# Sigmoid attention with mixture of depths on one core: rankings, choosing, turns, stores and weight loads given other places in a hand-written order

## The chip, the core and the metric

The kernel runs on one core of a Trainium2 chip. The core has a matrix engine (PE, with its weight loads shown apart as PEld), a vector engine (DVE), a scalar engine (ACT), a general engine (POOL), a queue engine for transfers (SP), and 16 DMA engines between on-chip memory and HBM. Each engine works through its own list of instructions strictly in the order written, and waits where an instruction needs what another engine or a transfer has not yet delivered. The metric is the device time in microseconds (us).

## What is computed

Inputs are q, k and v of shape (8, 12, 448, 64), a gate vector of 768 and two weights, 768 x 1024 and 1024 x 768. All is float32.

```python
scores = scale * np.matmul(q, k.transpose(0, 1, 3, 2)) - np.log(S)
attn = 1.0 / (1.0 + np.exp(-scores))
x = np.matmul(attn, v)             # then (B, H, S, D) -> (B, S, H*D)
scores = np.einsum('bsd,d->bs', x, w_gate)
out = x.copy()
for b in range(B):
    top_idx = np.argpartition(-scores[b], capacity)[:capacity]   # 128 of 448
    xe = x[b, top_idx]
    ye = np.maximum(xe @ w1, 0.0) @ w2
    g = 1.0 / (1.0 + np.exp(-scores[b, top_idx]))
    out[b, top_idx] = x[b, top_idx] + g[:, None] * ye
```

So each batch first needs its attention, then a score for each token, then the rank of each token, and only for the 128 best tokens the two layers.

## The kernel before

**Attention.** The 96 heads are worked in 12 units s = 0 to 11 of two groups of four heads. Three groups make a batch, so batch b is complete after unit (3b+2)//2, and `FULL[b]` names the unit after that one: 2, 3, 5, 6, 8, 9, 11, 12. Each unit has 7 slots n = 0 to 6. A slot (`slot`, L322, L351) scores two row blocks of its own unit into the banks PA (`a0`, `a1`), lets ACT squash them (`squash`, L336) into attn tiles, and beside this accumulates values (`value`) of slots 0 to 3 for the unit before it and of slots 4 to 6 for its own unit, into the banks PO (`o0`, `o1`). The last values of a unit fall in slot 3 of the next, and there DVE takes the result out of PO in four transposes (`takes`, L372). One round of values in a unit is odd: it holds two half rounds that write the same banks from different rows of the array, so that ACT puts a `join` (L359) between them. This is slot (s,3) from s = 4 on, and (s,2) for s = 1 to 3.

**Per batch.** After the takes, DVE multiplies and sums with the gate vector (`gate_part`, L380 and L383, for each group), `gate` (L398 to L413) makes the scores, and POOL sends them to HBM (L408). `spread` (L420, on POOL) brings them back as `rep`, the same row in all 128 partitions. `ranking` compares them (`rank`, L428 and L431, four blocks of tokens) and `place` (L441 to L456) builds a one-hot matrix, for batches 2 to 5 also sums of it. `choose` (L465, L469) multiplies that on PE, `fetch` (L476, L479) turns the answer into row numbers on DVE and starts the gather of 128 rows from `out` on POOL (L489). These rows must have been stored before: `store` (L389) writes x in four pieces of rows. `scatter` (L630) writes the finished rows back.

**The two layers.** They run for pairs of batches p. `turn_rows` (item `("t", b)`, L507 to L529) transposes the gathered rows. Each layer is done with 7 products instead of 8, on quarters of the weights and on sums of quarters: items `(1, p, key)` (`first`, L546, with sums on DVE or ACT at L559 to L565) and `(2, p, key)` (`second`, L610, with sums into the rows at L621); `("c", b)` is choose and fetch. Three quarters of each weight are held, the fourth and the four sums are made once (`make_sum`, L200), kept in HBM (L202) and lent again to a spare buffer when needed (`lend`, L225). The lists in `BLOCKS` say which items come after slot (s,3) of which unit; `block` hands each item a pair of banks or one half of a pair, two items in turn to each pair.

**Order.** The order is written out by hand: `after(s, n)` says what follows each slot, and every instruction is put on its engine's queue in that order. Buffers make the queues wait for each other. `raw_k` has one buffer, so the load of k 2s+4 waits until `turn` (L304) has turned k 2s+3. qT and kT have four buffers, so new ones wait until PE has finished an older unit. `rep` has one buffer, xe three. Loads (L101, L150, L177), lends, sums to HBM and stores all go through SP's one queue. After the last slot, `rest` does the remaining values, the last two batches and the last pair.

Of the kernel before, what the change touches and what calls it, by code (L numbers as in the profile page):

```python
# [17 lines left out]
def kernel(  # L18
# [161 lines left out]
    def load_held(m):  # L180
        for x, at in enumerate((HELD1, HELD2)[m - 1]):
            load_quarter(m, (w1_sb, w2_sb)[m - 1][:, x], at)
# [3 lines left out]
    def load_left(m):  # L186

        for n, x in ((1, "a"), (2, "b")):
            room[x] = spare(n)[:, :QW]
        load_quarter(m, room["a"], (1, 0) if m == 1 else (0, 1))  # L190

    def make_sum(m, key):
        a, b = room["a"], room["b"]
        w00, wx, w11 = [(w1_sb, w2_sb)[m - 1][:, x] for x in range(3)]
        dst, x, y, op = {
            (1, 5): (b, a, w11, ALU.add), (1, 7): (a, w00, a, ALU.subtract),
            (1, 6): (b, w11, a, ALU.subtract), (1, 3): (a, wx, b, ALU.subtract),
            (2, 5): (b, a, w00, ALU.subtract), (2, 7): (a, a, w11, ALU.subtract),
            (2, 6): (b, w00, a, ALU.subtract), (2, 4): (a, wx, b, ALU.subtract)}[m, key]
        nc.vector.tensor_tensor(out=dst, in0=x, in1=y, op=op)  # L200
        t = sums[m, key] = dram.tile([P, QW], F32, name=f"sum{m}{key}", bufs=1)
        nc.sync.dma_start(out=t, in_=dst)  # L202


    SUMS = {(1, 4): [(1, 5)], (1, 6): [(1, 7)], (2, 1): [(1, 6)], (2, 4): [(1, 3)],
            (4, 4): [(2, 5)], (4, 6): [(2, 7)], (5, 1): [(2, 6)], (5, 2): [(2, 4)]}
# [421 lines left out]
    def scatter(b):  # L628
# [8 lines left out]
        4: [("t", 0), (1, 0, 1), ("c", 1)],  # L637
        5: [("t", 1), (1, 0, 2), (1, 0, 6)],
        6: [(1, 0, 7), (1, 0, 4), (1, 0, 5), ("c", 2), (1, 0, 3), (2, 0, 1)],
        7: [(2, 0, 2), (2, 0, 4), (2, 0, 3), (2, 0, 5), (2, 0, 6), ("c", 3), ("t", 2)],  # L640
        8: [(2, 0, 7), ("t", 3), (1, 1, 1), (1, 1, 2), (1, 1, 6), (1, 1, 7), (1, 1, 4)],
        9: [(1, 1, 5), (1, 1, 3), (2, 1, 1), ("c", 4), (2, 1, 2), (2, 1, 4)],
        10: [(2, 1, 3), (2, 1, 5), (2, 1, 6), ("c", 5), (2, 1, 7), ("t", 4)],
        11: [(1, 2, 1), ("t", 5), (1, 2, 2)],
# [21 lines left out]
    def block(s):  # L666

        places = [("o0", 0), ("o0", 1), ("a1", 0), ("a1", 1), ("a0", 0), ("a0", 1),
                  ("o1", 0), ("o1", 1)]
        at = 0  # L670
        for i, item in enumerate(BLOCKS[s]):
            if item[0] == "t":
                at += at % 2
                turn_rows(item[1], banks(places[at % 8][0]))
                at += 2
            else:
                name, n = places[at % 8]
                ps = banks(name)[:, n]
                if item[0] == "c":
                    fetch(*choose(item[1], ps))  # L680
                else:
                    finish(item, begin(item, ps))
                at += 1
            if i == 1:
                turn("q", 2 * s + 2)
                turn("k", 2 * s + 3)
                load("k", 2 * s + 4)
            if i == 2:
                turn("q", 2 * s + 3)
# [36 lines left out]
    def slot(s, n):  # L726
# [11 lines left out]
        if split(vs, i):  # L738
            one, two, u = rounds(vs)[i]
            for e, p in ((0, one), (1, two)):  # L740
                for half in range(2):
                    if e == 0:
                        score(s, n, e, 1 - half, PA[1 - half])
                        value(vs, half, p, u)
                        join(half)
                    else:
                        value(vs, half, p, u)
                        score(s, n, e, 1 - half, PA[1 - half])
                        squash(s, n, 1 - half, PA[1 - half])
                        if i == 6:  # L750
                            takes(vs, half)
            return
        for half in range(2):
# [16 lines left out]
            if (s, n, half) == (FIRST - 1, NF + 1, 0):  # L770
                fetch(*choose(0, PO[1][:, 1]))

    FIRST = NG // 2 + 3

    def rest():
# [3 lines left out]
        ranking(B - 2)  # L779
# [56 lines left out]
    def after(s, n):  # L836

        if n == NF and s:
            if 4 < s:
                load_v(s)  # L840
            if s in BLOCKS:
                block(s)
            else:
                turn("q", 2 * s + 2)
                turn("k", 2 * s + 3)
                load("k", 2 * s + 4)
                turn("q", 2 * s + 3)
            gates(2 * s - 2)
            gates(2 * s - 1)
# [3 lines left out]
        if s == 0:  # L853
# [5 lines left out]
            if n == 3:  # L859
                load_held(1)  # L860
                load_left(1)
# [6 lines left out]
        if (s, n) in ((1, 4), (2, 6), (3, 4)):  # L868
            load_v({1: 2, 2: 3, 3: 4}[s])
        for key in SUMS.get((s, n), ()):  # L870
            make_sum(*key)
        if (s, n) == (4, 0):
            load_held(2)
            load_left(2)
        for b in range(B - 1):
            full = FULL[b]
            if (s, n) == (full, 5 + b % 2):
                spread(b)
            if (s, n) == (full, 6):
                store(b)  # L880
            if (s, n) == (full + 1, 1):
                ranking(b)
        if s == NS - 1:
# [3 lines left out]
            if n == 6:  # L887
                lend(2, 5, "heads")
                lend(2, 6, "heads")
                lend(2, 7, "attn")  # L890

# [55 lines left out]
```

## Time and profile before

The three runs took 543.79, 545.67 and 547.75 us, so the median is 545.67. The profiled execution took 542.69 us, of which its span on the core is 540.9.

| | busy us of 540.9 | share |
|---|---|---|
| PE | 456.9 | 84% |
| PE weight load | 258.6 | 48% |
| DVE | 305.3 | 56% |
| ACT | 188.4 | 35% |
| POOL | 33.2 | 6% |
| mean DMA, 84.67 MB | 157 GB/s | |
| granted PE clock, mean | 0.934 | |

The page gives busy shares; they are averages over stages with different limits. Where PE stands still is read from the list of waits and from the timelines: a line there has start and length in us, the engine, the line of the kernel, the operation with what it writes and reads, the number of instructions merged, and in brackets how long the engine was idle before and what ended that. The granted clock of PE is given for each stretch of time; 1.00 is full speed. Half speed makes a 2.7 us item of the first layer take 5.4.

### The profile page before, as it was taken

Reading aid. Unit: us, or ns where it says so; the run is one execution under the profiler, and the core shown is the slowest. Engines: PE = TensorE matmul, PEld = TensorE weight load, DVE = VectorE, ACT = ScalarE, POOL = GpSimd, SP = SyncE. Lnnn points to the kernel's source line nnn. Section 1 sums busy time; section 2 is a strip of 40 time slices with the busy share of each in tenths; the row PEclk is TensorE's granted clock in tenths of the full one; section 3 lists DMA queues with packets and bytes.
Section 4 is the critical chain, followed back from the end, with each engine's and each line's share of the span. In section 5 each row is a group of like instructions: output and inputs, shape, how many; then the busy total and the mean of one; then the engine's idle time right before and its main releaser. Section 6 shows DMA issues by size and latency. Waiting matters only on the chain.

```text
span 540.9 us, 14311 instructions
## 1 busy us (share of the span) xinstructions
PE 456.9 (84%) x6374; PEld 258.6 (48%) x6374; DVE 305.3 (56%) x643; ACT 188.4 (35%) x225; POOL 33.2 (6%) x55
## 2 busy tenths in 40 slices
PE   8999997089897967895899897769578999899995
PEld 3535332034546537332444842634134365877962
DVE  3329575626747584945542567446646065986462
ACT  4666663036362630351065055005402642000100
POOL 5000010010000000000000000000002000001001
PEclk9999998579899989997999999879978999799998
DMA  8986639799385892953643694158716378351001
GB/s 212 335 222 192 214 109 163 205 159 331 127 320 134 234 209 85 240 150 68 196 150 94 193 161 147 33 179 151 199 52 212 120 128 227 62 98 59 30 1 58
DMA packets 115726, 84.67 MB, mean 157 GB/s; under 512 B 90624, under 2 KB 99456, under 8 KB 115664
## 3 DMA queue, kind: packets, MB, share of 16 engines
q1 hardware_dynamic: 113680, 75.84, 53.3%
q0 software_dynamic: 1984, 7.91, 4.7%
q8 instruction: 50, 0.82, 0.6%
q14 instruction: 12, 0.10, 0.1%
HBM read 63.28 MB, written 20.46 MB: 155 GB/s over the span
## 4 chain that ended last, share of the span: by engine, by line
PE 56%; DVE 19%; DMA 10%; issue 7%; SPq 4%; ACT 2%; POOL 0%; POOLq 0%; DVEq 0%; ACTq 0%
PE a L322 14%; PE o L351 13%; PE o L546 8%; PE o L610 6%; PE a L546 6%; PE a L610 6%; DMA rep<-scores 4%; SPq L389 2%; DMA scores<-total 2%; DVE scr L431 2%; DVE scr L428 2%; ACT attn L336 2%; DVE hidden L559 2%; DVE x_b L372 2%; DVE xe L621 2%
## 5 line engine op out<-in xcount | busy, mean ns | idle before, releaser
L322 PE MATMUL a<-qT,kT 32*64 32x448 f32 x2624 | 256.5, 544 | 7.7 <-ACT attn L336 5.9
L336 ACT ACTIVATE attn<-a,bias_s 128x896 f32<-128x896 f32 x162 | 162.0, 1007 | 146.0 <-PE a L322 93.1
L351 PE MATMUL o<-attn,raw_v 32*64 32x448 f32 x2176 | 206.3, 541 | 0.2 <-issue 0.2
L322 PEld LDWEIGHTS a<-qT,kT 32*64 32x64 f32 x2624 | 92.1, 132 | 105.3 <-ACT attn L336 71.1
L351 PEld LDWEIGHTS o<-attn,raw_v 32*64 32x64 f32 x2176 | 73.6, 132 | 36.8 <-issue 30.2
L351 PE MATMUL o<-attn,rows_t 32*64 32x448 f32 x448 | 45.6, 565 | 19.8 <-DVE got L479 17.5
L372 DVE STREAM_TRANSPOSE x_b<-o 128x448 f32<-128x448 f32 x48 | 26.9, 616 | 43.2 <-PE a L322 33.1
L304 DVE STREAM_TRANSPOSE kT<-raw_k 128x448 f32<-128x448 f32 x42 | 24.2, 616 | 36.6 <-PE a L322 19.5
L428 DVE TENSOR_SCALAR_CACHE_REDUCE scr<-rep,who 128x448 f32<-128x448 f32 (+1 forms) x32 | 21.6, 676 | 33.4 <-DMA rep<-scores 32.5
L546 PE MATMUL o<-rows_t,spare 128*128 128x128 f32 x192 | 29.4, 323 | 10.3 <-DVE x_b L372 8.1
L562 ACT ACTIVATE hidden<-hidden 128x512 f32<-128x512 f32 x12 | 7.5, 630 | 80.1 <-DVE hidden L559 80.1
L546 PEld LDWEIGHTS o<-rows_t,spare 128*128 128x128 f32 x192 | 28.2, 236 | 12.2 <-DVE x_b L372 9.7
L351 PEld LDWEIGHTS o<-attn,rows_t 32*64 32x64 f32 x448 | 16.1, 136 | 31.3 <-DVE got L479 19.0
L296 DVE STREAM_TRANSPOSE qT<-qT 128x896 f32<-128x896 f32 x23 | 25.2, 1094 | 10.4 <-DMA qT<-in_q_dram 10.4
L383 DVE TENSOR_REDUCE gate_p<-scr 128x14 f32<-128x448 f32 x48 | 29.8, 621 | 1.7
L380 DVE TENSOR_TENSOR scr<-x_b,wg_b 128x448 f32<-128x448 f32 x48 | 29.7, 619 | 1.1
L610 PE MATMUL o<-w_sb,hidden 128*128 128x384 f32 x40 | 18.6, 621 | 12.7 <-DVE x_b L372 12.7
L621 DVE SCALAR_TENSOR_TENSOR xe<-a,gate,xe 128x384 f32<-128x384 f32 x32 | 18.1, 609 | 16.0 <-PE a L610 11.9
L510 ACT ACTIVATE rows_t<-o 128x768 f32<-128x768 f32 x4 | 3.2, 811 | 68.3 <-PE o L507 42.9
L559 DVE TENSOR_TENSOR hidden<-o,hidden 128x512 f32<-128x512 f32 x17 | 11.3, 687 | 24.6 <-PE o L546 24.5
L431 DVE SCALAR_TENSOR_TENSOR scr<-rep,who,earlier 128x448 f32<-128x448 f32 (+1 forms) x32 | 21.8, 683 | 1.4
L610 PE MATMUL a<-w_sb,hidden 128*128 128x384 f32 x56 | 21.3, 527 | 0.8 <-DVE hidden L559 0.8
(112 smaller groups left out, 417.2 us busy)
## 6 DMA issues: line engine op xcount, KB each, us to landing
spare<-sum SPq DMA_DIRECT2D x38, 384.0 KB, 4.4
qT<-in_q_dram SPq DMA_DIRECT2D x24, 448.0 KB, 6.2
out_dram<-x_b SPq DMA_DIRECT2D x32, 336.0 KB, 7.7
raw_k<-in_k_dram SPq DMA_DIRECT2D x22, 448.0 KB, 4.6
raw_v<-in_v_dram SPq DMA_DIRECT2D x36, 224.0 KB, 4.7
sum<-spare SPq DMA_DIRECT2D x8, 768.0 KB, 5.5
w_sb<-in_moe_w_dram SPq DMA_DIRECT2D x6, 768.0 KB, 10.3
rows_t<-in_v_dram SPq DMA_DIRECT2D x8, 224.0 KB, 10.6
```

Of the source, the lines that this page charges most:

```text
L296: nc.vector.transpose(heads["q", i], heads["q", i])
L322: nc.tensor.matmul(out[y * Dh:(y + 1) * Dh, h % 2, :S], kt[d, e, r:r + 2].rearrange("d r t -> d (r t)"), qt[d, e], start=(e == 0), stop=(e ...
L336: nc.scalar.activation(a, psc[:, :, :S], AF.Sigmoid, bias=bias_s, scale=QK_SCALE)
L351: nc.tensor.matmul(PO[x][j * Dh:(j + 1) * Dh, pr, :S], raw_v[s][rows, 2 * pr + j, at:at + Dh], attn[s, pr, n][rows, j, :], start=((s, x, p ...
L372: nc.vector.transpose(x_tiles[b][:, :, 2 * g + pr, :], PO[x][:, pr, :S].rearrange("p (r t) -> p r t", t=TT))
L380: nc.vector.tensor_tensor(out=tmp, in0=x_tiles[b][:, :, hp, :], in1=wg_b[:, hp:hp + 1, :].to_broadcast([P, TB, TT]), op=ALU.mult)
L383: nc.vector.tensor_reduce(out=gate_parts[b][:, :, hp], in_=tmp, axis=AX.X, op=ALU.add)
L428: nc.vector.tensor_scalar(out=junk[:n], in0=rep[:n], scalar1=own, scalar2=0.0, op0=ALU.is_gt, op1=ALU.add, accum_out=above[:n, c:c + 1])
L431: nc.vector.scalar_tensor_tensor(out=junk[:n], in0=rep[:n], scalar=own, in1=earlier[:n, c, :], op0=ALU.is_equal, op1=ALU.mult, accum_out=l ...
L546: nc.tensor.matmul(ps[:, f, :n], w((t * FH + f) * P, P), x[:, t, :n], start=(t == 0), stop=(t == KH - 1))
L610: nc.tensor.matmul(ps[:n, :DH], h[:, t, :n], w(t * DH, DH), start=(t == 0), stop=(t == FH - 1))
L621: nc.vector.scalar_tensor_tensor(out=xe[:n, cols], in0=ps[:n, :DH], scalar=st[b]["gate"][:n, 0:1], in1=xe[:n, cols], op0=ALU.mult, op1=ALU ...
```

## The change

`rounds` stay as they are, and so does all arithmetic. What moves:

- Batch 0 is chosen as the only item of block 4, no more inside slot (3,4). The items of blocks 4 to 11 are shifted by one or more places, most choosing to the block of the next unit.
- `RANKED` gives each ranking its slot: (4,1), (5,1), (6,1), (7,5), (9,1), (10,5), (11,6), where it was (3,1), (4,1), (6,1), (7,1), (9,1), (10,1) and the start of `rest`. The spread of batch 1 goes from (3,6) to (4,3).
- The turns of q and k for the next unit leave the inside of the block and come behind it. Gate parts, which all stood behind block and turns, now stand in three places: from units in FULL, the first goes ahead of the block; for units 6 and 9 the second goes ahead of the turns; the rest stays.
- `block` gives out banks from `a1` on, and a `t` takes the next pair that is wholly free.
- Stores go one piece at a time, two slots of a unit and two of the next (two each in (11,4) and (11,5) for batch 6). Weight quarters are loaded one at a time. A sum is made in one slot and sent to HBM one or two slots later. v of units 2 to 4 is loaded at slot 4 of the unit before.
- The odd round of a unit runs its first half for both banks, then all four groups of scores, then its second half, and only then the squashes and takes.

```diff
@@ -177,16 +177,15 @@
         nc.sync.dma_start(out=dst.rearrange("p (t c) -> p t c", t=KH if m == 1 else FH),
                           in_=quarter(m, *at))
 
-    def load_held(m):
-        for x, at in enumerate((HELD1, HELD2)[m - 1]):
-            load_quarter(m, (w1_sb, w2_sb)[m - 1][:, x], at)
+    def load_held(m, x):
+        load_quarter(m, (w1_sb, w2_sb)[m - 1][:, x], (HELD1, HELD2)[m - 1][x])
 
     room = {}
 
     def load_left(m):
 
         for n, x in ((1, "a"), (2, "b")):
-            room[x] = spare(n)[:, :QW]
+            room[x] = spare(n)
         load_quarter(m, room["a"], (1, 0) if m == 1 else (0, 1))
 
     def make_sum(m, key):
@@ -198,12 +197,20 @@
             (2, 5): (b, a, w00, ALU.subtract), (2, 7): (a, a, w11, ALU.subtract),
             (2, 6): (b, w00, a, ALU.subtract), (2, 4): (a, wx, b, ALU.subtract)}[m, key]
         nc.vector.tensor_tensor(out=dst, in0=x, in1=y, op=op)
-        t = sums[m, key] = dram.tile([P, QW], F32, name=f"sum{m}{key}", bufs=1)
-        nc.sync.dma_start(out=t, in_=dst)
-
-
-    SUMS = {(1, 4): [(1, 5)], (1, 6): [(1, 7)], (2, 1): [(1, 6)], (2, 4): [(1, 3)],
-            (4, 4): [(2, 5)], (4, 6): [(2, 7)], (5, 1): [(2, 6)], (5, 2): [(2, 4)]}
+        sums[m, key] = dst
+
+    def keep_sum(m, key):
+        t = dram.tile([P, QW], F32, name=f"sum{m}{key}", bufs=1)
+        nc.sync.dma_start(out=t, in_=sums[m, key])
+        sums[m, key] = t
+
+
+    MADE = {(2, 1): (1, 5), (2, 2): (1, 7), (3, 1): (1, 6), (3, 2): (1, 3),
+            (4, 5): (2, 5), (4, 6): (2, 7), (5, 1): (2, 6), (5, 2): (2, 4)}
+    KEPT = {(2, 2): (1, 5), (2, 4): (1, 7), (3, 2): (1, 6), (3, 4): (1, 3),
+            (4, 6): (2, 5), (5, 1): (2, 7), (5, 2): (2, 6), (5, 3): (2, 4)}
+    WEIGHTS = {(0, 6): (1, 0), (1, 1): (1, 2), (1, 2): (1, None), (1, 4): (1, 1),
+            (4, 0): (2, 0), (4, 1): (2, 2), (4, 2): (2, None), (4, 4): (2, 1)}
 
     def attn_tile(pr, n):
         return attnp.tile([P, 2, S], F32, name=f"attn{pr}_{n}")
@@ -634,14 +641,14 @@
 
 
     BLOCKS = {
-        4: [("t", 0), (1, 0, 1), ("c", 1)],
-        5: [("t", 1), (1, 0, 2), (1, 0, 6)],
-        6: [(1, 0, 7), (1, 0, 4), (1, 0, 5), ("c", 2), (1, 0, 3), (2, 0, 1)],
-        7: [(2, 0, 2), (2, 0, 4), (2, 0, 3), (2, 0, 5), (2, 0, 6), ("c", 3), ("t", 2)],
-        8: [(2, 0, 7), ("t", 3), (1, 1, 1), (1, 1, 2), (1, 1, 6), (1, 1, 7), (1, 1, 4)],
-        9: [(1, 1, 5), (1, 1, 3), (2, 1, 1), ("c", 4), (2, 1, 2), (2, 1, 4)],
-        10: [(2, 1, 3), (2, 1, 5), (2, 1, 6), ("c", 5), (2, 1, 7), ("t", 4)],
-        11: [(1, 2, 1), ("t", 5), (1, 2, 2)],
+        4: [("c", 0)],
+        5: [("t", 0), ("c", 1), (1, 0, 1), (1, 0, 2), ("t", 1), (1, 0, 6)],
+        6: [(1, 0, 7), (1, 0, 4), (1, 0, 5), (1, 0, 3), ("c", 2), (2, 0, 1)],
+        7: [(2, 0, 2), (2, 0, 4), (2, 0, 3), (2, 0, 5), (2, 0, 6), ("t", 2)],
+        8: [(2, 0, 7), ("c", 3), (1, 1, 1), (1, 1, 2), ("t", 3), (1, 1, 6), (1, 1, 7)],
+        9: [(1, 1, 4), (1, 1, 5), (1, 1, 3), ("c", 4), (2, 1, 1), (2, 1, 2), (2, 1, 4)],
+        10: [(2, 1, 3), (2, 1, 5), (2, 1, 6), (2, 1, 7), ("t", 4)],
+        11: [("c", 5), (1, 2, 1), (1, 2, 2), ("t", 5)],
     }
 
     LENT = {5: [(1, 6)], 6: [(1, 7), (1, 5), (1, 3)], 7: [(2, 4), (2, 5), (2, 6)],
@@ -665,28 +672,20 @@
 
     def block(s):
 
-        places = [("o0", 0), ("o0", 1), ("a1", 0), ("a1", 1), ("a0", 0), ("a0", 1),
-                  ("o1", 0), ("o1", 1)]
-        at = 0
-        for i, item in enumerate(BLOCKS[s]):
+        free = {name: [0, 1] for name in ("a1", "o0", "a0", "o1")}
+
+        def place(count):
+            name = next(x for x in free if len(free[x]) >= count)
+            taken, free[name] = free[name][:count], free[name][count:]
+            return banks(name) if count == 2 else banks(name)[:, taken[0]]
+
+        for item in BLOCKS[s]:
             if item[0] == "t":
-                at += at % 2
-                turn_rows(item[1], banks(places[at % 8][0]))
-                at += 2
+                turn_rows(item[1], place(2))
+            elif item[0] == "c":
+                fetch(*choose(item[1], place(1)))
             else:
-                name, n = places[at % 8]
-                ps = banks(name)[:, n]
-                if item[0] == "c":
-                    fetch(*choose(item[1], ps))
-                else:
-                    finish(item, begin(item, ps))
-                at += 1
-            if i == 1:
-                turn("q", 2 * s + 2)
-                turn("k", 2 * s + 3)
-                load("k", 2 * s + 4)
-            if i == 2:
-                turn("q", 2 * s + 3)
+                finish(item, begin(item, place(1)))
 
     def ranking(b):
         for c in range(NC):
@@ -737,18 +736,19 @@
         vs, i = (s, n - NF - 1) if n > NF else (s - 1, n + NF)
         if split(vs, i):
             one, two, u = rounds(vs)[i]
-            for e, p in ((0, one), (1, two)):
-                for half in range(2):
-                    if e == 0:
-                        score(s, n, e, 1 - half, PA[1 - half])
-                        value(vs, half, p, u)
-                        join(half)
-                    else:
-                        value(vs, half, p, u)
-                        score(s, n, e, 1 - half, PA[1 - half])
-                        squash(s, n, 1 - half, PA[1 - half])
-                        if i == 6:
-                            takes(vs, half)
+            for half in range(2):
+                value(vs, half, one, u)
+                join(half)
+            for e in range(2):
+                for pr in (1, 0):
+                    score(s, n, e, pr, PA[pr])
+            for half in (1, 0):
+                value(vs, half, two, u)
+            for pr in (1, 0):
+                squash(s, n, pr, PA[pr])
+            if i == 6:
+                for x in (1, 0):
+                    takes(vs, x)
             return
         for half in range(2):
             pr = 1 - half
@@ -767,16 +767,11 @@
             squash(s, n, pr, PA[pr])
             if i == 6:
                 takes(vs, half)
-            if (s, n, half) == (FIRST - 1, NF + 1, 0):
-                fetch(*choose(0, PO[1][:, 1]))
-
-    FIRST = NG // 2 + 3
 
     def rest():
 
 
         s = NS - 1
-        ranking(B - 2)
         for p, some in ((1, (4, 5, 6)), (0, (2, 3, 4, 5, 6))):
             if p == 0:
                 nc.tensor.drain()
@@ -836,17 +831,23 @@
     def after(s, n):
 
         if n == NF and s:
-            if 4 < s:
+            odd = s in FULL[1::2]
+            if s > 4:
                 load_v(s)
+            if odd or s in FULL:
+                gates(2 * s - 2)
             if s in BLOCKS:
                 block(s)
-            else:
-                turn("q", 2 * s + 2)
-                turn("k", 2 * s + 3)
-                load("k", 2 * s + 4)
-                turn("q", 2 * s + 3)
-            gates(2 * s - 2)
-            gates(2 * s - 1)
+            if odd and s > 3:
+                gates(2 * s - 1)
+            turn("q", 2 * s + 2)
+            turn("k", 2 * s + 3)
+            load("k", 2 * s + 4)
+            turn("q", 2 * s + 3)
+            if not odd and s not in FULL:
+                gates(2 * s - 2)
+            if not odd or s == 3:
+                gates(2 * s - 1)
         if n == NF + 1:
             for i, (m, key) in enumerate(LENT.get(s + 1, ())):
                 lend(m, key, i)
@@ -856,29 +857,32 @@
                 turn("q", 1)
                 load("k", 2, 3)
                 load("q", 2, 3)
-            if n == 3:
-                load_held(1)
-                load_left(1)
             if n == 4:
                 turn("k", 2, 3)
                 load_v(1)
                 load("k", 4)
             if n == 5:
                 turn("q", 2, 3)
-        if (s, n) in ((1, 4), (2, 6), (3, 4)):
-            load_v({1: 2, 2: 3, 3: 4}[s])
-        for key in SUMS.get((s, n), ()):
-            make_sum(*key)
-        if (s, n) == (4, 0):
-            load_held(2)
-            load_left(2)
+        if n == NF + 1 and 0 < s < 4:
+            load_v(s + 1)
+        if (s, n) in WEIGHTS:
+            m, x = WEIGHTS[s, n]
+            if x is None:
+                load_left(m)
+            else:
+                load_held(m, x)
+        if (s, n) in KEPT:
+            keep_sum(*KEPT[s, n])
+        if (s, n) in MADE:
+            make_sum(*MADE[s, n])
         for b in range(B - 1):
             full = FULL[b]
-            if (s, n) == (full, 5 + b % 2):
+            if (s, n) == ((4, 3) if b == 1 else (full, 5 + b % 2)):
                 spread(b)
-            if (s, n) == (full, 6):
-                store(b)
-            if (s, n) == (full + 1, 1):
+            for a, at in enumerate(((full, 5), (full, 6), (full + 1, 1), (full + 1, 2))):
+                if (s, n) == (at if b < B - 2 else (full, 4 + a // 2)):
+                    store(b, (a,))
+            if (s, n) == RANKED[b]:
                 ranking(b)
         if s == NS - 1:
             if n == 0:
@@ -888,6 +892,8 @@
                 lend(2, 5, "heads")
                 lend(2, 6, "heads")
                 lend(2, 7, "attn")
+
+    RANKED = [(4, 1), (5, 1), (6, 1), (7, 5), (9, 1), (10, 5), (11, 6)]
 
     def stream():
         for i in range(2):
```

## The prediction

> **What bounds the kernel now.** I read the page first: PE is busy 456.9 of 540.9 us, so at most 84 us of idle time are to be had, and what the low clock behind each gap costs. Then the list of waits, PE alone, longest first. Columns: total us, times, longest.
>
> ```profile
> PE o L351 <- DVE got L479: 17.5, 1, 17.5
> PE o L610 <- DVE x_b L372: 13.2, 3, 7.0
> PE a L465 <- DVE xe L621: 9.2, 3, 5.1
> PE o L546 <- DVE x_b L372: 8.7, 3, 4.1
> ```
>
> All of them are waits for DVE. For the first I read the timelines of DVE and SP around 90 us.
>
> ```profile
> 87.39 2.23 DVE L372 STREAM_TRANSPOSE x_b<-o 128x448 f32<-128x448 f32 x4
> 98.44 1.11 DVE L296 STREAM_TRANSPOSE qT<-qT 128x896 f32<-128x896 f32 x1 [8.81 <-DMA qT<-in_q_dram]
> 100.67 1.17 DVE L304 STREAM_TRANSPOSE kT<-raw_k 128x448 f32<-128x448 f32 x2 [1.12 <-DMA raw_k<-in_k_dram]
> 110.68 0.15 DVE L479 COPY got<-o 128x1 f32<-128x1 f32 x1
> ...
> 76.75 0.33 SPq L202 DMA_DIRECT2D sum<-spare  x1
> 80.20 12.16 SPq L389 DMA_DIRECT2D out_dram<-x_b  x4
> 92.45 3.15 SPq L101 DMA_DIRECT2D qT<-in_q_dram  x2
> 95.72 6.48 SPq L101 DMA_DIRECT2D raw_k<-in_k_dram  x2
> ```
>
> SP stood behind a weight sum until 76.75, then issued four stores for 12.16 us; only then came the loads of q and k, whose turns DVE holds ahead of the fetch of batch 0, and PE needs that fetch inside slot (3,4). For the x_b waits I read all engines at block 6:
>
> ```profile
> 189.96 0.68 DVE L428 TENSOR_SCALAR_CACHE_REDUCE scr<-rep,who 128x448 f32<-128x448 f32 x1 [4.94 <-DMA rep<-scores]
> 199.40 2.23 DVE L372 STREAM_TRANSPOSE x_b<-o 128x448 f32<-128x448 f32 x4
> 200.62 4.29 PE L546 MATMUL o<-rows_t,spare 128*128 128x128 f32 x24 [4.15 <-DVE x_b L372]
> 204.96 1.29 DVE L559 TENSOR_TENSOR hidden<-o,hidden 128x512 f32<-128x512 f32 x2 [3.33 <-PE o L546]
> 206.30 2.94 PE L546 MATMUL o<-rows_t,w_sb 128*128 128x128 f32 x24 [1.38 <-DVE hidden L559]
> ```
>
> The ranking starts when rep lands (189.96) and lasts 9.45 us to the takes; the takes free o0, the block's first bank. The last row shows a second thing: (1,0,4) goes to the other half of o0 and still starts 0.05 us after DVE has read (1,0,7) from the first half. 170.42, 213.38, 217.61 and 255.53 repeat it: the second item on a pair of banks waits for the readers of the first.
>
> **Parts and their costs.** T is the end of PE's work in slot (s,3). Before, T is 86.6 at s=3, 133.8, 165.0, 196.5, 243.7, 292.2, 334.6, 387.0, 434.8 at s=11. Durations from rows: turns of q, k, q 3.1 us; a gate part 2.6 (4 x 0.66); a whole gate() 2.6 more (177.62 to 180.25); ranking with place 9.45, or 6.7 where sums are not added; four takes 2.23; a fetch 0.3; first 2.7, second 2.6 at full clock; turn_rows 0.7.
>
> *Stores, weights, choosing at s=2 to 4.* Only two stores (6 us by the 12.16 of four) now stand before the loads of (3,0), the sum's DMA no longer holds SP at (2,4), and the fetch of batch 0 moves to block 4. A k load that is late is then first missed by PE at (4,0), 9 us after T. On SP turn k7 (T(2)+8.7, behind gates(2)) frees load k8, then come load_v(3), a sum and two stores (to about T(2)+17), the q loads and, 4 us before T(3), load k9: landed at T+1 to T+4, turned by T+7. T(3) to T(4) took 47.2; 3+3 plain slots of 3.02 and a split one give 21.8. Gain 25 us. Ahead of it, (3,0) waits perhaps 0.65 for q7, turned behind gates(2).
>
> *Odd unit in full rounds.* Before, slot (s,3) took 4.0 against 3.0: its second score group waits for the previous squash of PA[0] (0.42 shown idle at 193.96). In the new order one value round (0.75) runs first, but half the array still waits for the same squash. I get 3.75: 0.25 gained, 11 times; bounds -0.3 and 1.0. The takes then end at T+1.45.
>
> *Blocks.* Turns leave (3.1 us of DVE), but at s = 5, 8, 11 a gate part and a gate (5.2), at 6 and 9 a gate part (2.6) step ahead of the block's first read. The first bank is now a1, freed by ACT. Walking PE and DVE down each list:
> - 4: choose 0.8, then its pair a1 is needed by the next score, and the fetch sits behind takes: 1.8 in all (8.7 before; its items move to 5).
> - 5: between T(4) and T(5), some 24 us, DVE now has a fetch at 1.75, turns 3.1, two gate parts 5.2, four sums of w2 at 1.76, a turn of k 1.1 and ranking(1) 6.7: it comes free 1.4 us after T. Takes end T+3.6, gates 8.85, fetch(1) 9.15. c1 waits to 3.6, (1,0,1) on its pair to 9.2, (1,0,6) 2.4 for the differences of t1, now just ahead of it. 23 (9.1 before).
> - 6: ranking(2) is done before T, so the x_b wait (4.15) is gone; (1,0,4) waits 2.75 for gates(10), (1,0,3) 1.6, (2,0,1) 3.5 for the fetch behind 2.8 us of hidden sums. 24.9, plus 1.8 at (7,0), whose turns come after gates(11): 26.7 (24.0).
> - 7: nothing on DVE ahead; ranking(3) is at (7,5), choosing in 8. 15.3 (26.6: 5.67 for x_b, low clock after it, 1.81 at c3).
> - 8: c3 waits from 2.6 to 7.85; its gather has scatter(1) ahead on POOL, t3 to about 18; (1,1,6) 2.4 for t3. 28 (19.4, which held (1,1,4) too).
> - 9: waits 2.15 and 2.5; 24.5 (30.4, with 3.99 and 5.08).
> - 10: 13.8 (25.8: 6.99 and 2.28 gone).
> - 11: (1,2,1) shares a1 with c5, whose fetch is at T+7: 15.7 (6.9).
>
> Sums: 149 after, 151 before. The blocks only trade places. Each stall of over 2.2 us carries 1.5 to 2.5 us of low clock in this count.
>
> Here a rule is weighed. The clock rows (us, busy PE, PEld, DVE, ACT, POOL, PEclk, DMA, GB/s):
>
> ```profile
> 406.00:407.00 1.00, 0.00 (x0) 0.00 (x0) 1.00 (x3) 0.00 (x0) 0.57 (x1) 1.00 0.87 163
> 409.00:410.00 1.00, 1.00 (x3) 0.46 (x2) 0.00 (x0) 0.00 (x0) 0.00 (x0) 0.50 0.46 191
> 463.00:464.00 1.00, 1.00 (x7) 1.00 (x6) 1.00 (x3) 0.00 (x0) 0.00 (x0) 0.50 0.00 0
> ```
>
> Gaps of 2.28 (before 407.25) and 2.39 us (before 462.63) halved the clock for 2.9 and 5.9 us; 1.81 us (before 268.98) did not. The Trainium skill, "TensorE: Matmul & The Clock Gate", What's actually happening, asks for an idle window of about 3.4 us. By it the new gaps of 2.4 to 2.75 in 5, 6, 8 and 9 would cost nothing more, some 5 us less in all. The rows decide. A second rule speaks for more gain: "PSUM — Partial Sum Buffer", PSUM bank collisions, guards by bank and quadrant and calls different banks safe. If the waits went by bank, the second items would not wait, and walking the lists so takes 31 us off (6, 10.8, 1.5, 1.5, 6.8, 2.7, 1.7 in blocks 5 to 11): 480. The five starts above are against it.
>
> *End.* gates(20) move ahead of block 11, so ranking(6) is over 5 us before PE asks for it: 2.39 of waiting and 3.0 of half clock (462.9 to 468.9) go, 5.4.
>
> *Moved on the queues.* On SP the load of k waits for the turns behind the block, and the lends, two stores, the q loads and the next k stand behind it (some 20 us of issue and waits). load_v(7) and load_v(10) come 5 to 6 us after T and land near T+11 to T+16, needed at T+15.3 and T+13.8: I add 1 us, bounds 0 and 8. On POOL the gather of batch 3 is moved past scatter(1) (counted above), spread(1) behind gather(0), with 6 us to spare. Weight pieces at s=0 to 1: PE was full there, nothing gained; without its cover each piece is a landing of about 10 us.
>
> **Sum.** 540.9 less 25.3 (s=3), 2.2 (blocks), 1.8 (splits from s=4), 5.4 (end), plus 1 (v): 507 span, 509 with the 1.8 us around it. The profiled execution, 542.69, is 3 us below the median 545.67, so I say 511 on that scale.
>
> **Rivals.** (a) Forecast, chance 0.62: 490 to 531 by itself; the walk has some 60 us of stalls in it, and a third of them wrong is 20. (b) Fewer waits in the blocks (by bank, or DVE ahead of my count), 0.08: 480. (c) Same gain, but late landings eat some: k9 10 us later at (4,0) with 2 of clock, and both v 4 late: 20 more, 531, in 525 to 538; 0.18. For it: rows_t<-in_v takes 10.6 us to land; against: the SP walk leaves margins. (d) Slower, 0.07: the SP chain of turn, k, lends, stores, q, k becomes the bound. Its place is the first slot that needs v or the turned k after blocks 5 to 10. Margins there are about 2.5 us; if each of six units ran 9 us late, it is 6 x 6.5 = 39 and 2 of clock each: 51 less 35 gained, 561. It decides from 6 us late per unit. For: four stores alone held SP for 12 us; against: split in pairs, with 9 us of slots between. (e) Gain and loss cancel, 0.05: 541 to 551. That nothing changes is excluded, since the fetch leaves slot (3,4) for good.
>
> The range 490 to 538 leaves out b, d and e, 0.20. A measurement here tells 1% from no change. Faster by over 1%: 0.88; within: 0.05; slower: 0.07.
>
> **What would show it.** Right: no PE wait over 3 us between 70 and 105; no x_b wait ahead of blocks 6, 7, 9 and 10; block 7 near 15 us and block 10 near 14; PE waits for a fetch of 5 us or more at the start of 5, 8 and 11. Wrong: those last three missing (b), or PE waits at (s,4) for raw_v, or at (s,0) for turns of several us (c, d). If blocks 5, 8 and 11 lose more than 35 us over my count, the forecast fails altogether.

## The result, and the profile after

The changed kernel takes 530.69 us (526.86 to 532.33, four runs), before 544.73 in the same comparison: ratio 0.972, 95% interval 0.966 to 0.979. It is faster by some 14 us; 34 were forecast. The profiled execution took 530.28, its span is 528.5 against 540.9, 12.4 less.

The page after, busy time and the first lines of the slices:

```profile
PE 459.6 (87%) x6374; PEld 268.3 (51%) x6374; DVE 304.9 (58%) x643; ACT 187.4 (35%) x225; POOL 32.9 (6%) x55
PE   7999999989417997799997779879989779999995
PEclk9999999979857898799999799989999969999999
DMA  8977369999931596138984209911997492651001
```

The slices before had a hole in PE at 90 to 110 us; now it stands at 135 to 155, behind some 60 us in which the DMA engines are full. The list of waits of PE after (the lines have moved by some seven: L379 takes, L472 and L476 choose, L486 the end of a fetch, L553 first and L617 second layer, L566 and L628 their sums on DVE, L199 a sum of weights, L204 its way to HBM, L177 a load of a quarter, L396 a store):

```profile
PE o L476 <- DVE x_b L379: 15.3, 1, 15.3
PE a L553 <- DVE got L486: 6.6, 1, 6.6
PE a L472 <- DVE xe L628: 5.3, 1, 5.3
PE a L553 <- DVE hidden L566: 4.5, 2, 2.6
PE a L617 <- DVE xe L628: 3.9, 3, 2.4
PE o L553 <- DVE got L486: 3.5, 1, 3.5
```

The 17.5 us for `got` inside slot (3,4) are gone and so are the waits for x_b at blocks 6, 7, 9 and 10. But one wait of 15.3 us for x_b has come, nearly as large as the one removed. To see where the gain stands, stage by stage, this is the first score of slot (s,4), right behind block s, in both traces (us from the start):

| first score of | before | after | ahead |
|---|---|---|---|
| (4,4) | 141.35 | 112.08 | 29.3 |
| (5,4) | 174.15 | 174.30 | -0.2 |
| (6,4) | 220.38 | 222.71 | -2.3 |
| (7,4) | 270.23 | 262.12 | 8.1 |
| (8,4) | 311.63 | 312.37 | -0.7 |
| (9,4) | 364.90 | 358.27 | 6.6 |
| (10,4) | 412.83 | 394.58 | 18.2 |
| (11,4) | 441.64 | 434.74 | 6.9 |
| end | 540.9 | 528.5 | 12.4 |

The lead of the start is gone after block 5. About half of that was planned, since the items of block 4 were moved into block 5 and a time of 23 us for it was forecast; it took 37.5. Over the whole trace the start gains 25.5 us, blocks 4 to 11 together lose 15.1 (a gain of 2 was forecast), the slots between them lose 3.5, and the end gains 5.5. Two links from the chain of waits of the changed kernel before block 5 (start, length, what):

```profile
113.34 16.20 DMA spare<-in_moe_w_dram
131.43 9.03 DMA sum<-spare
```

The fourth quarter of w2 takes 16.20 us to land. Only then can DVE make two sums; the third writes the buffer of the first and waits until that has gone to HBM, 9.03 us. Ranking(1), the fourth sum and the takes of (5,3), which free o0 for c1, queue behind. Picked from DVE's timeline and from PE's:

```profile
129.64 3.55 DVE L199 TENSOR_TENSOR spare<-spare,w_sb 128x1536 f32<-128x1536 f32 x2 [5.92 <-DMA spare<-in_moe_w_dram]
140.55 1.76 DVE L199 TENSOR_TENSOR spare<-w_sb,spare 128x1536 f32<-128x1536 f32 x1 [6.28 <-DMA sum<-spare]
150.48 2.23 DVE L379 STREAM_TRANSPOSE x_b<-o 128x448 f32<-128x448 f32 x4
152.86 1.84 PE L476 MATMUL o<-who,hot 128*128 128x2 f32 x8 [15.28 <-DVE x_b L379]
```

T(5), the end of PE's work in slot (5,3), is 136.78: the takes begin 13.7 us after it, and c1 waits for them. SP's timeline shows what stands around the late landing: two pieces of a store hold SP for 7.51 us, and the issue of the fourth quarter for 10.71, while the share of the DMA engines is 1.02 (113 to 124 us).

```profile
100.37 7.51 SPq L396 DMA_DIRECT2D out_dram<-x_b  x2
113.34 10.71 SPq L177 DMA_DIRECT2D spare<-in_moe_w_dram  x1
124.78 4.82 SPq L101 DMA_DIRECT2D raw_k<-in_k_dram  x1
```

### The profile page after: what moved, and what is told of

It is laid out like the page before. It is cut to its first block, busy times and chain, and to the rows that moved or that the text cites. A ratio compares the mean times of both kernels' runs of the same rounds, so it can differ in the third digit from the quotient of the medians.

```text
span 528.5 us, 14342 instructions
## 1 busy us (share of the span) xinstructions
PE 459.6 (87%) x6374; PEld 268.3 (51%) x6374; DVE 304.9 (58%) x643; ACT 187.4 (35%) x225; POOL 32.9 (6%) x55
## 2 busy tenths in 40 slices
DMA packets 115726, 84.67 MB, mean 160 GB/s; under 512 B 90624, under 2 KB 99456, under 8 KB 115664
## 4 chain that ended last, share of the span: by engine, by line
PE 71%; DVE 14%; DMA 9%; issue 3%; ACT 2%; SPq 0%; POOLq 0%; DVEq 0%; ACTq 0%
PE a L329 21%; PE o L358 19%; PE o L553 9%; PE a L617 8%; PE a L553 7%; PE o L617 6%; DMA raw_k<-in_k_dram 3%; DMA spare<-in_moe_w_dram 3%; DVE x_b L379 2%; DMA sum<-spare 2%; DVE xe L628 2%; DVE hidden L566 1%; ACT attn L343 1%; DVE scr L387 1%; DVE scr L438 1%
## 5 line engine op out<-in xcount | busy, mean ns | idle before, releaser
L329 PE MATMUL a<-qT,kT 32*64 32x448 f32 x2624 | 249.5, 543 | 3.0 <-issue 1.4
L358 PE MATMUL o<-attn,raw_v 32*64 32x448 f32 x2176 | 202.0, 543 | 0.1
L358 PEld LDWEIGHTS o<-attn,raw_v 32*64 32x64 f32 x2176 | 75.3, 133 | 37.5 <-issue 30.5
L379 DVE STREAM_TRANSPOSE x_b<-o 128x448 f32<-128x448 f32 x48 | 27.1, 619 | 44.2 <-PE o L358 27.0
L311 DVE STREAM_TRANSPOSE kT<-raw_k 128x448 f32<-128x448 f32 x42 | 24.2, 615 | 28.1 <-DMA raw_k<-in_k_dram 16.6
L617 PE MATMUL a<-w_sb,hidden 128*128 128x384 f32 x64 | 26.4, 563 | 5.7 <-DVE got L486 3.3
L387 DVE TENSOR_TENSOR scr<-x_b,wg_b 128x448 f32<-128x448 f32 x48 | 29.3, 611 | 1.0
L566 DVE TENSOR_TENSOR hidden<-o,hidden 128x512 f32<-128x512 f32 x16 | 10.7, 688 | 33.0 <-PE o L553 32.9
L628 DVE SCALAR_TENSOR_TENSOR xe<-a,gate,xe 128x384 f32<-128x384 f32 x30 | 17.1, 611 | 21.2 <-PE a L617 21.0
L553 PE MATMUL o<-rows_t,spare 128*128 128x128 f32 x192 | 23.1, 277 | 5.1 <-DVE rows_t L526 2.9
L553 PE MATMUL o<-rows_t,w_sb 128*128 128x128 f32 x168 | 23.8, 307 | 4.3 <-DVE got L486 3.5
L553 PE MATMUL a<-rows_t,w_sb 128*128 128x128 f32 x120 | 18.4, 324 | 9.2 <-DVE got L486 6.6
L553 PEld LDWEIGHTS o<-rows_t,w_sb 128*128 128x128 f32 x168 | 23.0, 222 | 4.8 <-issue 3.6
L553 PEld LDWEIGHTS o<-rows_t,spare 128*128 128x128 f32 x192 | 22.1, 192 | 5.7 <-DVE rows_t L526 3.1
L566 DVE TENSOR_TENSOR hidden<-a,hidden 128x512 f32<-128x512 f32 x16 | 10.7, 687 | 24.1 <-PE a L553 23.9
L553 PE MATMUL a<-rows_t,spare 128*128 128x128 f32 x144 | 20.0, 303 | 4.9 <-DVE rows_t L526 2.9
```

The costliest lines, as they stand in the source:

```text
L311: nc.vector.transpose(kt[:, e], t[:, e].rearrange("p (a n) d -> p n a d", a=2))
L329: nc.tensor.matmul(out[y * Dh:(y + 1) * Dh, h % 2, :S], kt[d, e, r:r + 2].rearrange("d r t -> d (r t)"), qt[d, e], start=(e == 0), stop=(e ...
L358: nc.tensor.matmul(PO[x][j * Dh:(j + 1) * Dh, pr, :S], raw_v[s][rows, 2 * pr + j, at:at + Dh], attn[s, pr, n][rows, j, :], start=((s, x, p ...
L379: nc.vector.transpose(x_tiles[b][:, :, 2 * g + pr, :], PO[x][:, pr, :S].rearrange("p (r t) -> p r t", t=TT))
L387: nc.vector.tensor_tensor(out=tmp, in0=x_tiles[b][:, :, hp, :], in1=wg_b[:, hp:hp + 1, :].to_broadcast([P, TB, TT]), op=ALU.mult)
L553: nc.tensor.matmul(ps[:, f, :n], w((t * FH + f) * P, P), x[:, t, :n], start=(t == 0), stop=(t == KH - 1))
```

## The experiments

Each ratio is to the kernel before on the same chip; the changed kernel's is 0.972. The experiments ran on four chips, on which the kernel before had medians of 541 to 547 us, so differences between runs of different groups are good to a few us. **Theory W**: the sums of w2, which wait for transfers, stand ahead of the takes of (5,3). **Theory D** adds its cause: the DMA engines are full from unit 3 to block 5. **Rival G**: the gate work ahead of the blocks is what costs. **Theory P** is of the other blocks: the second item on a pair of banks waits for the readers of the first.

**1. The sums of w2 left out.**

```diff
-        nc.vector.tensor_tensor(out=dst, in0=x, in1=y, op=op)
+        if m == 1:
+            nc.vector.tensor_tensor(out=dst, in0=x, in1=y, op=op)
+        else:
+            dst = a
```

> Leaves out the four vector-engine sums of the second weight; their transfers to HBM stay, taken from the fourth quarter as loaded. Theory W (the changed kernel is 19 us behind my count at block 5 because DVE stands still for transfers in front of the sums, 5.9 us for the fourth quarter and 6.3 us for a sum on its way to HBM, with ranking(1) and the takes of slot (5,3) queued behind): the 15.3 us wait of PE for the takes falls under 3, block 5 takes about 23 us as counted, and the time falls by 14 to 19 us, to 512 to 517. Rival G (the gate work that now stands ahead of the block is what costs): DVE reaches the takes earlier, but c1 and (1,0,1) wait for the gate all the same, and the time falls by less than 6.

519.65 us, ratio 0.951 (0.944 to 0.958). The wait falls from 15.3 to 7.1 us, not under 3. G is refuted as the main cause at block 5; W holds for about half. The top of the list of DVE's waits between 100 and 170 us in this run (total, times, longest), and two lines of SP's timeline, say what took the other half:

```profile
DVE kT L314 <- DMA raw_k<-in_k_dram: 13.1, 3, 8.3
113.28 10.46 SPq L177 DMA_DIRECT2D spare<-in_moe_w_dram  x1
124.47 4.02 SPq L101 DMA_DIRECT2D raw_k<-in_k_dram  x1
```

DVE no longer waits for a sum, but for the load of k (8.3 us), which stands on SP behind the issue of the fourth quarter. That fits D: a landing is late here too.

**2. Ranking(1) ahead of the sums.**

```diff
-    RANKED = [(4, 1), (5, 1), (6, 1), (7, 5), (9, 1), (10, 5), (11, 6)]
+    RANKED = [(4, 1), (4, 4), (6, 1), (7, 5), (9, 1), (10, 5), (11, 6)]
```

> Ranking of batch 1 in slot (4,4), ahead of the sums of the second weight, and nothing else. Theory W: the ranking fits into the time in which DVE stood still for the fourth quarter, so DVE comes free some 6 us earlier at slot (5,3), since the wait for the sum on its way to HBM stays; time falls by 5 to 8, to 523 to 526. If the sums' waits are not what holds the takes: no change (530 to 532).

528.03, ratio 0.966 (0.960 to 0.972). 5 to 8 us were expected, and the median says 3, so this is hardly apart from nothing: the expectation is missed. The wait falls only from 15.3 to 12.5, since DVE now waits twice for a sum on its way to HBM, 4.7 us before the third sum and 3.6 before the fourth. The ranking was not the load; the waits around it were.

**3. Held quarters of w2 loaded early.**

```diff
-            (4, 0): (2, 0), (4, 1): (2, 2), (4, 2): (2, None), (4, 4): (2, 1)}
+            (1, 6): (2, 0), (2, 0): (2, 2), (2, 1): (2, 1), (4, 0): (2, None)}
```

> The three held quarters of the second weight are loaded in units 1 and 2 instead of unit 4, where the DMA engines are full from 105 to 150 us; the fourth quarter comes first in unit 4. Theory W with full DMA engines as its cause: the fourth quarter lands about 5 us earlier, the sums start earlier, the takes of (5,3) come 4 to 8 us earlier, time 522 to 527. If it is the wait of the one buffer for the sum's own transfer and not the load: under 3 us gained.

523.54, ratio 0.958 (0.950 to 0.967), and the wait 10.9. The same loads, moved out of the full stretch, give some 7 us, as D says. The fourth quarter is also issued earlier in the unit here, so the run does not part traffic from order; the sums begin 3 us earlier (126.67 against 129.64), where 5 were expected. SP's timeline holds a surprise: the quarter itself now holds SP for 0.39 us, and the two pieces of a store behind it for 10.40.

```profile
113.33 0.39 SPq L177 DMA_DIRECT2D spare<-in_moe_w_dram  x1
113.77 10.40 SPq L396 DMA_DIRECT2D out_dram<-x_b  x2
```

**4. Pairs of banks in turn.**

```diff
-        free = {name: [0, 1] for name in ("a1", "o0", "a0", "o1")}
+        order = iter({4: "a1", 5: "a1 o0 a0 a1 o1 o0", 6: "a1 o0 a0 o1 a1 o0",
...
+                      11: "a1 o0 a0 o1"}[s].split())
...
-            name = next(x for x in free if len(free[x]) >= count)
+            name = next(order)
```

> The items of a block take the pairs of banks in turn (a1, o0, a0, o1, then the second halves) instead of filling one pair after the other; order of items unchanged. Theory P (the second item on a pair waits for the readers of the first): the waits of 2.58, 3.31, 5.29, 2.38 and 6.63 us at blocks 6, 8, 9 and 11 go or shrink to under 2, and the low clock behind them; 15 to 25 us gained, 506 to 516, less what t3 and t5 then wait for their gathers. Rival (these waits are DVE being late and do not depend on the banks): under 4 us gained.

509.69, ratio 0.935 (0.928 to 0.941). Block 6 takes 14.6 us, 26.1 in the changed kernel, and block 9 16.4 instead of 23.9. Its PE timeline in block 6 has no gap at these items any more:

```profile
191.96 2.94 PE L553 MATMUL a<-rows_t,spare 128*128 128x128 f32 x24
194.74 2.84 PE L553 MATMUL o<-rows_t,w_sb 128*128 128x128 f32 x24
197.42 2.84 PE L553 MATMUL a<-rows_t,spare 128*128 128x128 f32 x24
```

P holds. The same instructions with the same DVE work ahead, and each starts as the last ends. Block 8 gains nothing (28.1), since t3 then waits for its gather, 7.7 us. Block 5 still takes 32.9, with 14.5 of it for the takes.

**5. The start undone.**

```diff
-    RANKED = [(4, 1), ...
+    RANKED = [(3, 1), ...
...
+            if (s, n, half) == (3, 4, 0):
+                fetch(*choose(0, PO[1][:, 1]))
...
-        4: [("c", 0)],
+        4: [],
```

> Only the start undone: ranking(0) back in (3,1), the choosing of batch 0 back inside slot (3,4); stores and sums stay in single pieces. My count: the fetch stands behind the turns, which end at 94.8 us in the changed kernel, and behind gates(5), so PE waits in (3,4) from about 91 to 100; block 4 then costs nothing. If the pieces did most of the work, the wait is 6 to 10 us and the time rises by 4 to 10 (535 to 541). If it was the place of the choosing alone, the wait is 15 us or more and the time is that of before, 544.

528.82, ratio 0.971 (0.963 to 0.979): not slower at all. The expectation is missed. PE waits 3.1 and 5.2 us in (3,4), but then only 3.8 for the takes at block 5, and the first squash of (5,4) comes at 178.84, against 176.53 in the changed kernel. T(4) comes 18 us later than in the changed kernel (126.8 against 108.3), and in that time the transfers catch up. DVE no longer waits for the fourth quarter, only 1.72 us for a sum's way to HBM, and its takes begin 2.2 us after T(5) (150.60):

```profile
142.89 1.76 DVE L199 TENSOR_TENSOR spare<-w_sb,spare 128x1536 f32<-128x1536 f32 x1 [1.72 <-DMA sum<-spare]
152.82 2.23 DVE L379 STREAM_TRANSPOSE x_b<-o 128x448 f32<-128x448 f32 x4
```

So the place of the choosing brings nothing to the end as long as the transfers ahead of the takes are not done: PE may stand in (3,4) or in block 5.

**6. Sums early.**

```diff
-    MADE = {(2, 1): (1, 5), (2, 2): (1, 7), (3, 1): (1, 6), (3, 2): (1, 3),
-            (4, 5): (2, 5), (4, 6): (2, 7), (5, 1): (2, 6), (5, 2): (2, 4)}
+    MADE = {(1, 5): (1, 5), (1, 6): (1, 7), (2, 0): (1, 6), (2, 1): (1, 3),
+            (3, 2): (2, 5), (4, 4): (2, 7), (4, 5): (2, 6), (5, 2): (2, 4)}
...
-            (4, 0): (2, 0), (4, 1): (2, 2), (4, 2): (2, None), (4, 4): (2, 1)}
+            (1, 6): (2, 0), (2, 0): (2, 2), (2, 1): (2, 1), (2, 5): (2, None)}
```

`KEPT` moves with it.

> Sums of the first weight in units 1 and 2, held quarters of the second in units 1 and 2, its fourth quarter in (2,5) and its first sum in (3,2): the same instructions and bytes, moved out of the stretch in which the DMA engines are full. Theory D (the stretch from unit 3 to block 5 is now paced by the DMA engines, and DVE, with the takes behind it, waits for their landings): the wait for the takes at block 5 falls from 15.3 to under 6, time 512 to 519. If a single landing was at fault, as in the run with the held quarters early, it stays near 523.

522.17, ratio 0.961 (0.952 to 0.969). The wait for the takes at block 5 falls from 15.3 to 1.1 us, as D says. But a sum placed at (2,1) waited for its buffer ahead of the takes of (2,3), and PE lost 5.95 us there; T(4) came 8.4 us later than in the changed kernel, and the time missed the upper end by 3. The same fault at another place.

**7. Gates behind the blocks.**

```diff
-            if odd or s in FULL:
-                gates(2 * s - 2)
             if s in BLOCKS:
                 block(s)
+            if s in FULL and s > 3:
+                gates(2 * s - 2)
```

with the second gate part always behind the turns, and units 2 and 3 unchanged.

> Gates of units 5, 6, 8, 9, 11 behind the block, turns after them. By my count of the blocks: the waits of 3.5 (block 5), 2.58 (6), 5.29 (8) and 6.63 (11) shrink, 15 to 20 us with the low clock; but scores and rep of batches 2 and 4 come later, so rankings (6,1) and (9,1) run into the takes and PE waits 3 to 6 us for x_b at blocks 6 and 9. Sum: 515 to 528. If the rankings lose all of it, 530 or more.

520.53, ratio 0.954 (0.946 to 0.961). The wait in block 11 falls from 6.6 to 1.3 and that of block 8 from 5.3 to 1.3, while no wait for x_b comes back at blocks 6 and 9. The wait for the takes at block 5 stays (17.4), and one of 3.5 us for a ranking comes in `rest`. So the gates ahead of blocks cost some 10 us of their own, apart from W.

**8. The odd slot in its old order** (the four lines of `slot` as before).

> The odd slot in its old order, nothing else. By my count 0.25 us for each of 11 slots, and some 0.5 at the start of 8 blocks where a1 is now free at once: 3 to 7 us slower, 533 to 538. If the full rounds bring nothing: 530 to 532.

531.85, ratio 0.975 (0.967 to 0.983): 1 us apart from the changed kernel, below what can be told. 3 to 7 us slower were expected; the full rounds bring nothing that can be told.

**9. Everything together, and the parts of it.** Run f1 has the edits of 4 and 6 (with one sum moved behind the takes of (2,3), the fourth quarter of the second weight loaded in (3,1) and its sums made from (4,2) on), and in blocks 5, 8 and 11 the choosing first and the gates right behind its fetch:

```diff
-        8: [(2, 0, 7), ("c", 3), (1, 1, 1), ...
+        8: [("c", 3), (2, 0, 7), (1, 1, 1), ...
...
                 fetch(*choose(item[1], place(1)))
+                if s in (5, 8, 11):
+                    gates(2 * s - 2)
```

> Three edits together: sums and weights early (with one sum behind the takes of (2,3), since it held them for 6 us when it was ahead); pairs of banks in turn; in blocks 5, 8 and 11 the choosing first and the gates right behind its fetch, at 6 and 9 the gates behind the block. If the three causes are separate: from 510 (pairs alone) the wait of 14.5 us for the takes at block 5 goes with its low clock (12 to 16), and the waits of 7.7 and 5.4 us of t3 and t5 for their gathers shrink to under 3 (8 to 10): 484 to 494. If the transfers of units 3 to 5 set the pace whatever the order, the end of block 5 stays where it is and the sum is 500 or more.

475.71 (472.14 to 481.49), ratio 0.874 (0.867 to 0.881). It is the fastest run here by far, below what was expected. Its page:

```profile
PE 444.8 (93%) x6374; PEld 257.4 (54%) x6374; DVE 304.2 (64%) x643; ACT 187.6 (39%) x225; POOL 33.4 (7%) x55
DMA packets 115726, 84.67 MB, mean 178 GB/s; under 512 B 90624, under 2 KB 99456, under 8 KB 115664
```

PE spends 12 us less in the same 6374 records than before, at a mean clock of 0.978 against 0.934. Bytes and packets are those of before: only their order differs. The DMA engines are nearly as full as in the changed kernel, with a share of 0.95 from 86.6 us to T(5), against 0.99 there. So full engines are not what costs time; it costs where an instruction ahead of the takes waits for a landing.

f2 has pairs and early sums, without the new place of choosing and gates:

> Pairs of banks in turn, and sums and weights early; the gates stay ahead of the blocks. If the wait for the takes at block 5 was the transfers ahead of the sums, it falls under 3 us as it did in the run with early sums, and the time to 495 to 502; t3 and t5 still wait 7 and 5 us for their gathers.

498.88, ratio 0.922 (0.914 to 0.931); the wait for the takes is 1.8, t3 and t5 wait 7.7 and 5.3.

g1 is f1 with sums and weights where the changed kernel has them:

> As the run with all three, without the early sums and weights. If the sums that stand ahead of the takes of (5,3) are a cause of their own, the wait of 12 to 15 us at block 5 comes back, and the time is 12 to 18 above 476: 488 to 494. If the gates ahead of the block were what held the sums and takes up, it stays under 482.

490.42, ratio 0.904 (0.899 to 0.910). 14.0 us of waiting at block 5 are back (c1 comes first here and waits for ranking(1), which stands behind the sums), and 14.7 us of time, or some 17 by the ratios: the sums and the weights they need are a cause of their own. g2 is f2 with one quarter (768 KB) loaded three more times:

```diff
+            (4, 0): (2, 1), (4, 1): (2, 1), (3, 6): (2, 1)}
```

> As the run with pairs in turn and early sums (498.9), with one held quarter of the second weight (768 KB) loaded three more times in (3,6), (4,0) and (4,1): the same instructions on the compute engines, and the traffic of unit 4 about what the changed kernel had. Theory D (full DMA engines are what made the landings late): the wait for the takes at block 5 rises from 1.8 to 6 us or more, time 504 to 512. Rival (only the order counts, sums that wait for their own buffers ahead of ranking and takes): the wait stays under 4, time 498 to 502.

508.00, ratio 0.939 (0.933 to 0.944). More transfers, with nothing else changed, are enough to bring the wait back, as D says. The two lines are from the DVE timelines of f2 and of g2, the sum that waits for its buffer:

```profile
125.83 1.76 DVE L199 TENSOR_TENSOR spare<-w_sb,spare 128x1536 f32<-128x1536 f32 x1 [2.85 <-DMA sum<-spare]
```

```profile
135.78 1.76 DVE L199 TENSOR_TENSOR spare<-w_sb,spare 128x1536 f32<-128x1536 f32 x1 [11.78 <-DMA sum<-spare]
```

With 2.3 MB more traffic in unit 4, the wait grows from 2.85 to 11.78 us, the wait of PE for the takes from 1.8 to 12.4, and the time by 9. The compute engines have the same instructions. The extra loads stand both on the DMA engines and in SP's one queue, ahead of the sums; which of the two makes the landing late is not parted by this run, nor by any other here.

## Why the prediction fell short

The direction and the mechanisms of the blocks held; the forecast was 511 and the range 490 to 538 holds 530.69, but less than half of the gain came.

**The step that failed** is the one on block 5: "it comes free 1.4 us after T", where "it" is DVE. It summed the work of DVE between T(4) and T(5), 24 us of it, and no waits for the transfers that this work needs. Of the 37.5 us of block 5, 23 were counted. DVE began the takes 13.7 us after T instead of 1.4, with 12.2 us spent waiting for the fourth quarter (5.92) and for a sum's way to HBM (6.28). Runs 1, 6, g1 and g2 show it from four sides, and run 5 shows that the sum of DVE's work itself was right: with the transfers done, the takes began 2.2 us after T. Behind it lies an omission: some 20 us of standing still at the start had been time in which the transfers could catch up. Once PE no longer stood there, the stores of two batches, w2, sums, q and k fell into a shorter stretch. From 86.6 us, which is T(3) in both traces, to T(5) the DMA engines had a share of 0.77 over 78.4 us before, and of 0.99 over 50.2 us after. Forecast rival (c), late landings, had the right kind of cause and the wrong place: k9 and v were only a little late.

**The rest of what is missing.** Of a gain of 33.7 us in the span 12.4 came, so 21.3 are missing. Block 5 holds 14.5 of them and block 4 1.9. Most of the rest lies in the slots between the blocks: from the first score behind block 4 to T(11), without the blocks, they took 158.3 us before and 161.8 after, where 0.8 less had been forecast. (The last step of the forecast's sum gives 512 and not 511: 507.2, 1.8 and 3.0. Nothing hangs on it.)

**Where the count held.** T(4) was forecast 25.3 ahead, at 108.5; it came at 108.33. The time of each block from T to the next score:

| block | before | forecast | after |
|---|---|---|---|
| 4 | 7.5 | 1.8 | 3.7 |
| 5 | 9.1 | 23 | 37.5 |
| 6 | 23.9 | 24.9 | 26.1 |
| 7 | 26.6 | 15.3 | 15.7 |
| 8 | 19.4 | 28 | 27.8 |
| 9 | 30.3 | 24.5 | 23.9 |
| 10 | 25.8 | 13.8 | 14.2 |
| 11 | 6.8 | 15.7 | 15.6 |

Blocks 6 to 11 are within 1.2 us each, and with them the waits that were named: 6.63 us at block 11, 5.29 at c3, 3.31 at (2,0,1). Block 4 is 1.9 over, because DVE finished ranking(0) 1.4 us after T(4): it had begun behind the turn of a k that landed at 101.67.

**Pairs of banks.** The rule of the Trainium skill that different banks are safe ("PSUM — Partial Sum Buffer", PSUM bank collisions) was set aside for five rows of the trace. Run 4 shows that this was right: with the same work, spread over pairs, the waits are gone. The rule is not contradicted: each pair of banks is one tile in the kernel, and the trace reads these waits from its semaphores, so that it is the program that guards by pair.

**The odd slot** was counted at 0.25 us of gain, 11 times. From the start of the last plain squash to T it took 3.57 us before and 3.54 after at s = 5, and run 8 gives 1 us in all. PE's list did lose its waits for `attn` at the scores, 5.9 us in all before and 0.4 after, but the slots became no shorter for it.

**The low clock.** Gaps of 2.38 and 2.58 us were followed by items at 4.19 and 4.57 us instead of 2.6 to 2.9, as the forecast had it from the rows of before; by the idle window of about 3.4 us in the Trainium skill ("TensorE: Matmul & The Clock Gate", What's actually happening) they would have cost nothing more. But one gap of 2.89 (before 305.77) was followed by full speed. And after block 4, two gaps of 1.58 and 0.59 us, with only the eight small products of c0 between them, were followed by half speed from 112 to 116 us (columns as in the forecast):

```profile
112.00:116.00 4.00, 3.92 (x48) 1.55 (x56) 1.14 (x2) 0.44 (x1) 1.63 (x2) 0.50 0.99 340
```

So the length of one gap does not decide. In each of the 14 traces all changes of the clock lie on a grid of 3.41 us, which agrees with the length of the skill's window. Cut on that grid, a piece at full clock in which PE was busy for less than 0.40 of the time was followed by half clock in 86 of 86 cases, and one with 0.75 or more in none; between, both occur. The piece need not be idle: a gap of 2.4 us that falls into one piece leaves 0.30 of it at most, while the gap of 2.89 fell across two, of 0.45 and 0.70, and the piece with c0's first gap had 0.54. (The two stretches of half clock that the forecast gives as 2.9 and 5.9 us lasted one and two such pieces, 3.4 and 6.8.) For block 4 the forecast counted no low clock at all: the slots from (4,4) to (5,3) took 24.7 us, the next five such stretches 22.0 to 23.7.

**The end** was counted at 5.4; from the first score of (11,4) it took 99.3 before and 93.8 after, 5.5 less. **v** was counted at 1 us; slots (10,4) to (11,3) took 24.5 against 22.0, with 1.4 us of waiting for raw_v in (10,4) seen by the weight loads; the rest stays open.

What was not tried is a smaller number of bytes, stores in longer runs, or loads on another queue than SP's; that the 128-byte runs of the stores are what fills the engines is argued from rates alone.

## What to carry to other kernels

When a stall is removed, ask what had been catching up in it: sum the transfers of the shorter stretch as well as the work of the engines, and ask which of them an instruction ahead of the bottleneck's buffers waits for. On an engine that works in order, count for every instruction what it waits for, and put those that wait for transfers behind those that free the bottleneck's buffers. Where small items share a buffer that is guarded as a whole, give them out in turn over all buffers; here this was worth more than the whole change.

## What the runs showed of the hardware

Issuing a transfer is not always quick, and the one that is issued need not be the cause. The same quarter of w2 held SP for 10.71 us in the changed kernel, behind two other quarters and a piece of a store, and for 0.39 us in run 3, where it came first and the two pieces of a store behind it held SP for 10.40; before, four loads of quarters took 3.1 us to issue at a DMA share of 0.96 (122 to 126 us). That SP is held by what is still under way, and not by the transfer that it issues, fits these numbers but was not tested. The busy share of the DMA engines says little about bytes. Between 80 and 100 us, with stores, 0.92 of their time moved 213 GB/s, and between 140 and 145 us 1.04 moved 427. Of 115726 packets 90624 are under 512 bytes. The mean granted clock was 0.934 before, 0.937 after, and 0.978 in f1, where PE's longest gap between start and end is 2.9 us. Its changes lie on a grid of 3.41 us, and how long PE was busy within one such piece goes before them, as shown above.
